# Counting two token tiles in one matmul inside a greedy expert search, on one Trainium2 core

## The chip, the cores and the metric

The kernel runs on one core of one Trainium2 chip. The metric is the device time of one launch in microseconds (us). TensorE (PE) runs matmuls, VectorE (DVE) and ScalarE (ACT) move and combine data, GpSimd (POOL) issues the gathers and scatters, SyncE (SP) the weight loads.

## The reference

```
def _attn_ref(q, k, v):            # B, H, S, D = 4, 8, 768, 64
    ...                            # window of 16 around each token, and 24 block summaries
    return np.matmul(a, v_all)

def _moe_ref(x, w_gate, w1, w2):   # N, D, E, F = 3072, 512, 8, 1024
    cap = N // E
    logits = x @ w_gate
    flat = logits.flatten()
    order = np.argsort(-flat)
    for idx in order:
        tok, e = (int(idx) // E, int(idx) % E)
        if assigned[tok] >= 0 or counts[e] >= cap:
            continue
        assigned[tok] = e
        counts[e] += 1
        ...
    for e in range(E):
        mask = assigned == e
        h = np.maximum(x[mask] @ w1[e], 0.0)
        out[mask] = h @ w2[e]
```

Attention feeds a gate. The gate hands all token and expert pairs out in the order of their logits until each of the 8 experts has its 384 tokens. Then each expert runs its two layers over its tokens.

## The kernel before

**Stages.** Attention with the logits takes the first 133 us. Then the greedy assignment is done in eight rounds (`route`, rounds 0 to 7): each round finds the next expert that fills up, and which tokens it gets. Round 0 runs alone, ahead of the first expert. Rounds 1 to 7 are interleaved with the matmuls of experts 0 to 5.

**A search.** A round (but for the last) finds the key at which the first expert is full, digit by digit: `search` runs twice, three digits each, so six digits a round and 42 in all. For one digit, VectorE compares the keys of the 24 tiles of 128 tokens with `n` (32 or 64) pivots into `g` (line 106). TensorE counts: for each tile one matmul with 128 columns of `g` as weights and the tile's one-hot experts `oh` (8 columns) as the moving operand, all 24 added up in PSUM `pc` (line 467), pivots on partitions, experts on columns. VectorE marks what has reached the capacity, with the row's maximum beside it, in `full` (line 469), a product with `steps` (line 472) turns this into the next digit, and VectorE makes the next pivots `piv` (line 476) and `g`. After the six digits come `inc`, a prefix product (lines 540 and 541), `span`, a product that lists the tokens (line 572), and `idx`, the list from which GpSimd gathers the tokens' rows (line 623, tile `xg`).

**An expert.** First 96 matmuls `h` of 128x384 (line 778): eight slices `f`, each of three groups of four, the first group with `xh` and `ah`, the second with `xh` and `al`, the third with `xl` and `ah`. Then 72 matmuls `y` of 128x512 (line 795). An operand is split in two halves so that two fast products carry its precision: `ah` and `bh` by ScalarE from the weights `raw` (line 609), `al` and `bl` by VectorE (line 612), likewise `xh` (ScalarE, line 643) and `xl` (VectorE, line 646) from the gathered rows, which TensorE transposes first (line 134, three matmuls of one of four parts `d`; below "a flip"). `hh` and `hl` (lines 782 and 785) are the halves of `h`. The flips and `h` share a pool of four PSUM buffers, so slice 0 of an expert takes the buffer of flip 0 and waits until `xh` and `xl` of part 0 have been read from it. The first `h` group of slice 0 needs `xh` of all four parts, the third group `xl` of all four.

**Order.** The program is written out by one loop over the matmuls, which keeps an estimated time `now` and an estimate of when VectorE will be free. A search step `yield`s two numbers, its cost to `now` and the time VectorE needs before the next step may be written; `vector` adds the latter to VectorE's estimate, to which the splits add theirs, and `service` writes the next step after the first matmul at which the estimate has passed. `prepare` writes the next expert's splits and flips between the `y` matmuls (`q` counts them in threes, 1 to 24): a flip once a set time has gone by since the gather, or from `q` = 22, and at `q` = 24 all that is left. All engines run their own instructions in the written order.

```
    def vector(cost):
        state["dve"] = max(state["dve"], state["now"] + TUNE["hop"]) + TUNE["dv"] * cost
        return state["dve"]
...
        if q and p["a"] < 4 and p["w"] is not None and now >= p["last"] and (q > TUNE["ql"] or now >= p["w"] + TUNE["aw"] + TUNE["as_"] * p["a"]):
            split_w(r, "a", p["a"])
...
        elif q > TUNE["qf"] and p["d"] < 4 and p["x"] is not None and (q > TUNE["ql"] or now >= max(p["x"] + TUNE["xw"], p["flip"])):
            flip_x(r, p["d"])
```

Of the kernel before, what the change touches and what calls it, by code (L numbers as in the profile page):

```python
# [8 lines left out]
F32 = mybir.dt.float32  # L9
F32R = mybir.dt.float32r  # L10
BF = mybir.dt.bfloat16
# [4 lines left out]
OP = mybir.AluOpType  # L16
AX = mybir.AxisListType
# [3 lines left out]
BLK, WIN, E, F, DM = 32, 16, 8, 1024, 512  # L21
N = B * S
CAP = N // E
# [9 lines left out]
NT = N // 128  # L33
VD = D + 1
TUNE = dict(
    hop=0.22, dv=1.0, e5=2, e50=0, warm2=3.6192, adv=14, y0=2.6, y1=0.3, y2=0.45,
    y2m=0.021, y3=1.7, y4=1.5, y5=1.6, y7=1.1, lo=1.1, sp=1.6, qx=23.421, aw=9.0, as_=2.6,
    ap=1.6, qf=8.3981, xw=5.4012, fp=2.4, ql=21.2102, mm=0.174, my=0.228, wlo=1.6, xlo=1.1, LA=6.154, PT=7, 
    sm=4, spe=0.015, sdve=0.316, sact=0.358, spool=0, m=0.569, e=2.793, t=2.307, c=0.793,
    n=0.518, xt=3.377, xf=3.104, l=5.806, k=18.109, q=16.26, vm=5, mx=12.906, back=6.52, w=5.302, qa=-11.877, qb=1.082, cut=22,  # L40
# [15 lines left out]
def attention_moe(ctx, tc, qT, kT, v65, wg, w1r, w2r, cst, out, dbg=None, dbi=None):  # L56
    nc = tc.nc
# [18 lines left out]
    rt = ctx.enter_context(tc.tile_pool(name="rt", bufs=1))  # L76
# [15 lines left out]
    HT = NT // 2  # L92
# [5 lines left out]
    def steps_tile():  # L98
        G.append(G.pop(0))
        return G[-1]  # L100

    def compare(g, dup, piv, n, t0=0, t1=NT):
        for k in range(2):
            a, b = max(t0, k * HT), min(t1, (k + 1) * HT)
            if a < b:
                nc.vector.tensor_tensor(g[k][:, (a - k * HT) * n:(b - k * HT) * n].rearrange("p (t j k) -> p t j k", k=2, j=n // 2),  # L106
                                        dup[:, a:b, None].to_broadcast([128, b - a, n // 2, 2]),
                                        piv[:, None, :n].to_broadcast([128, b - a, n]).rearrange("p t (j k) -> p t j k", k=2), op=OP.is_ge)
# [71 lines left out]
    with ExitStack() as att:  # L180
# [134 lines left out]
        for u in range(U):  # L315
            b, i = divmod(u, NQ)
            t, s = divmod(u, 2)
# [56 lines left out]
        for t in range(NT):  # L374
# [63 lines left out]
            if t + 1 in cuts:  # L438
                k = cuts.index(t + 1)
# [19 lines left out]
    nc.gpsimd.tensor_tensor(slot, ids_b[:, :3, 0], ids_b[:, :3, 1], op=OP.add)  # L459
    nc.gpsimd.tensor_scalar(slot, slot, 1.0, None, op0=OP.add)  # L460

    def search(R, oh, dup, g, digits):
        below = -32768.0 - 65536.0 / digits[0]
        for i, n in enumerate(digits):
            pc = R[:, :E]
            for t in range(NT):
                nc.tensor.matmul(pc, g[t // HT][:, t % HT * n:t % HT * n + 128], oh[:, t], start=t == 0, stop=t == NT - 1)  # L467
            full = rt.tile([128, E + 1], BF, name="full", bufs=2)
            nc.vector.tensor_scalar(full[:, :E], pc, CAP - 0.5, 0.0, op0=OP.is_ge, op1=OP.max, accum_out=full[:, E:])
            yield 0.027 * NT, TUNE["y1"]  # L470
            ps = R[:, 16:17 + E]
            nc.tensor.matmul(ps, steps[:, STEP[digits][i]], full, start=True, stop=True)
            if i < 2:
                m = digits[i + 1]
                piv = rt.tile([128, 64], I16, name="piv", bufs=2)
                nc.vector.tensor_scalar(piv[:, :m], offs[:, FROM[digits][i]:FROM[digits][i] + m], ps[:, E:], below, op0=OP.add, op1=OP.add)
                g = steps_tile()
                compare(g, dup, piv, m)
                below = rt.tile([128, 1], F32, name="below", bufs=2)
                nc.vector.tensor_scalar(below, piv[:, :1], -STEPS[STEP[digits][i + 1]][0], None, op0=OP.add)  # L480
                yield 0.03, TUNE["y2"] + m * TUNE["y2m"]
        return (below, ps[:, E:]), ps[:, :E], ps[:, E:]
# [3 lines left out]
    def route(r):  # L486
# [11 lines left out]
        if r < E - 1:  # L498
            at, won, top = yield from search(R, oh, T["dup"], T["g"], T["digits"])
            d = rt.tile([128, NT], F32, name="d", bufs=2)  # L500
            nc.vector.tensor_scalar(d, halves[:, :, 1], *at, op0=OP.subtract, op1=OP.subtract)
            nc.vector.scalar_tensor_tensor(d, d, 65536.0, halves[:, :, 0], op0=OP.mult, op1=OP.add)
            dup2 = rt.tile([128, NT, 2], I16, name="dup", bufs=2)
            nc.vector.tensor_scalar(dup2, d[:, :, None].to_broadcast([128, NT, 2]), 32767.0, -32768.0, op0=OP.min, op1=OP.max)
            g = steps_tile()
            compare(g, dup2, piv0, 32)
            wh = rt.tile([128, E], F32, name="wh", bufs=2)
            nc.vector.scalar_tensor_tensor(wh, won, top, w8f, op0=OP.is_equal, op1=OP.mult)
            yield 0.03, TUNE["y3"]
            at, won, top = yield from search(R, oh, dup2, g, EVEN)  # L510
            wl = rt.tile([128, E], F32, name="wl", bufs=2)
            nc.vector.scalar_tensor_tensor(wl, won, top, wh, op0=OP.is_equal, op1=OP.mult)
            nc.vector.tensor_scalar(d, d, *at, op0=OP.subtract, op1=OP.subtract)
            nc.vector.tensor_reduce(w, wl, axis=AX.X, op=OP.max)
            sel = rt.tile([128, NT], F32, name="sel", bufs=2)
            nc.vector.tensor_scalar(sel, tgt, w, None, op0=OP.is_equal)
            nc.vector.tensor_scalar(widx, w[:1], -512.0, 512.0 * E, op0=OP.mult, op1=OP.add)
            nc.vector.scalar_tensor_tensor(ge[:, 0], d, 0.0, sel, op0=OP.is_gt, op1=OP.mult)
            nc.vector.scalar_tensor_tensor(ge[:, 1], d, 0.0, sel, op0=OP.is_equal, op1=OP.mult)
        else:  # L520
            nc.vector.tensor_scalar(w, wsum, -1.0, float(E * (E + 1) // 2), op0=OP.mult, op1=OP.add)
            nc.vector.tensor_scalar(ge[:, 0], tgt, w, None, op0=OP.is_equal)
            nc.vector.tensor_scalar(widx, w[:1], -512.0, 512.0 * E, op0=OP.mult, op1=OP.add)
            nc.vector.memset(ge[:, 1], 0.0)
# [350 lines left out]
```

## Time and profile before

| | us |
|---|---|
| median of 3 runs | 487.07 (486.86 to 488.96) |
| the profiled execution | 486.22 |
| span of its instructions | 484.5 |
| TensorE busy | 451.9 |
| VectorE busy | 335.0 |

The span runs from the first instruction to the last; 1.7 us of the execution lie around it. Busy time of TensorE is from modelled ends, so a matmul that waits inside a stream can still be counted as busy. A row of the timeline gives the start, the duration, the engine and line, and in brackets the idle time of the engine before it and what ended it; rows of one kind that follow each other are merged with their count, and then the duration runs from the first start to the last end.

### The profile page before, as it was taken

To read this page: it belongs to the slowest core of one execution; us is meant where nothing else is said; L and a number is where in the kernel's file an instruction comes from. 1 tells how busy PE (TensorE), PEld (TensorE's weight loads), DVE (VectorE), ACT (ScalarE), POOL (GpSimd) and SP (SyncE) were. 2 spreads that over 40 slices of the span, in tenths; PEclk is the share of its full clock that TensorE was granted. 3 is DMA by queue.
4 is the path that set the end of the run, shared out by engine and by line. 5 is a ranking of instruction groups with operands and counts; after the bars stand their busy time and mean duration, and the time that the engine had idled before them with its cause. 6 is when DMAs were issued, how large, how long until landed. Compare 5 with 4: busy or idle time off the path is not lost.

```text
span 484.5 us, 13157 instructions
## 1 busy us (share of the span) xinstructions
PE 451.9 (93%) x5159; PEld 382.8 (79%) x5159; DVE 335.0 (69%) x1307; ACT 215.1 (44%) x449; POOL 126.6 (26%) x209
## 2 busy tenths in 40 slices
PE   6999999999946899999989999999999999999992
PEld 5686877878835797798779779878878988989981
DVE  5989889869768877768858947876877661562500
ACT  3886877858401432433234324514342453443400
POOL 2597839224113001300221112104101302202010
PEclk9999999999955999999999999999999999999998
DMA  8998392211204704703715606605525662621001
GB/s 303 410 330 312 118 375 84 78 46 67 90 3 141 272 2 167 277 37 141 271 68 179 236 23 227 229 2 200 195 86 197 179 225 99 174 85 66 0 23 43
DMA packets 22429, 73.38 MB, mean 151 GB/s; under 512 B 3168, under 2 KB 3424, under 8 KB 21984
## 3 DMA queue, kind: packets, MB, share of 16 engines
q1 hardware_dynamic: 16608, 53.67, 31.6%
q0 software_dynamic: 5760, 18.88, 11.1%
q8 instruction: 41, 0.67, 0.6%
q14 instruction: 20, 0.16, 0.1%
HBM read 59.95 MB, written 12.58 MB: 150 GB/s over the span
## 4 chain that ended last, share of the span: by engine, by line
PE 75%; DVE 11%; issue 7%; DMA 2%; POOL 2%; SPq 1%; ACT 1%; POOLq 0%; DVEq 0%; ACTq 0%
PE y L795 23%; PE h L778 22%; PE o L366 5%; PE r L467 5%; PE t L134 5%; PE s L330 4%; PE x L134 3%; PE l L372 3%; PE h L134 2%; DMA vw<-v 1%; DVE g L106 1%; POOL out L761 1%; DVE bl L612 1%; DMA xg<-xd,idx 1%; PE x L272 1%
## 5 line engine op out<-in xcount | busy, mean ns | idle before, releaser
L795 PE MATMUL y<-bl,hh 128*128 128x512 f32 x192 | 77.9, 406 | 0.0
L795 PE MATMUL y<-bh,hh 128*128 128x512 f32 x192 | 77.0, 401 | 0.0
L795 PE MATMUL y<-bh,hl 128*128 128x512 f32 x192 | 76.4, 398 | 0.0
L761 POOL DMA_INDIRECT out<-y,idx x24 | 24.1, 1006 | 181.5 <-ACT y L759 175.1
L782 ACT ACTIVATE hh<-h 128x384 fp32r<-128x384 f32 x64 | 31.5, 492 | 88.3 <-PE h L778 86.8
L778 PE MATMUL h<-xh,ah 128*128 128x384 f32 x256 | 57.2, 341 | 0.9 <-DVE xl L749 0.9
L345 ACT ACTIVATE pe<-sm,mx 128x120 f32<-128x120 f32 x192 | 57.9, 386 | 0.3 <-DVE mx L338 0.2
L778 PE MATMUL h<-xl,ah 128*128 128x384 f32 x256 | 57.8, 341 | 0.0
L778 PE MATMUL h<-xh,al 128*128 128x384 f32 x256 | 57.1, 340 | 0.0
L785 DVE SCALAR_TENSOR_TENSOR hl<-h,hh 128x384 fp32r<-128x384 f32 x64 | 35.1, 551 | 29.2 <-ACT hh L782 28.4
L623 POOL DMA_INDIRECT xg<-xd,idx x24 | 23.7, 987 | 106.8 <-issue 79.6
L609 ACT ACTIVATE ah<-raw 128x1024 fp32r<-128x1024 f32 (+1 forms) x36 | 32.7, 958 | 34.6 <-DMA raw<-w1r 33.9
L778 PEld LDWEIGHTS h<-xh,ah 128*128 128x128 f32 x256 | 45.0, 188 | 2.2 <-DVE xl L749 1.1
L778 PEld LDWEIGHTS h<-xl,ah 128*128 128x128 f32 x256 | 45.0, 188 | 2.1 <-issue 1.6
L643 ACT ACTIVATE xh<-h 128x384 fp32r<-128x384 f32 x28 | 13.7, 492 | 72.1 <-PE h L134 72.0
L778 PEld LDWEIGHTS h<-xh,al 128*128 128x128 f32 x256 | 45.1, 188 | 0.0
L338 DVE CUSTOM_DVE_ANT_0 sm<-s,cs 128x120 f32<-128x120 f32 x192 | 41.2, 278 | 4.8 <-PE s L330 4.3
L467 PEld LDWEIGHTS <-g 128*128 128x128 bf16 x1008 | 28.7, 97 | 18.4 <-DVE g L106 7.7
L795 PEld LDWEIGHTS y<-bh,hh 128*128 128x128 f32 x192 | 36.2, 188 | 6.5
L795 PEld LDWEIGHTS y<-bl,hh 128*128 128x128 f32 x192 | 36.2, 188 | 6.0 <-issue 0.5
L795 PEld LDWEIGHTS y<-bh,hl 128*128 128x128 f32 x192 | 36.2, 189 | 5.8
L467 PE MATMUL r<-oh,g 128*128 128x8 bf16 x1008 | 32.5, 167 | 7.3 <-DVE g L106 3.8
(137 smaller groups left out, 790.9 us busy)
## 6 DMA issues: line engine op xcount, KB each, us to landing
raw<-w1r SPq DMA_DIRECT2D x32, 512.0 KB
raw<-w2r SPq DMA_DIRECT2D x32, 512.0 KB, 4.3
kd<-kT SPq DMA_DIRECT2D x16, 400.0 KB, 5.4
vw<-v SPq DMA_DIRECT2D x24, 260.0 KB, 7.5
xd<-x POOLq DMA_DIRECT2D x24, 256.0 KB
qt<-qT SPq DMA_DIRECT2D x3, 1536.0 KB
qt<-qT SPq DMA_DIRECT2D x3, 512.0 KB
xg<-xd,idx POOLq DMA_INDIRECT x24
```

What stands on the lines that cost most here:

```text
L134: nc.tensor.transpose(o, i, idn)
L338: nc.vector.tensor_tensor_reduce(sm[:, p], PS[u][:, p], m, -0.125, 3e38, op0=OP.add, op1=OP.min, accum_out=mx[:, p:p + 1])
L345: nc.scalar.activation(PE_[u][:, p], SM[u][0][:, p], AF.Exp, bias=SM[u][1][:, p:p + 1], scale=-1.0)
L366: nc.tensor.matmul(po(t, s)[x * 64:x * 64 + 64, p], PT[u][:, p, x * 64:x * 64 + 64], VW[b % 2][:C, i - s + x, 2 * p + s], start=True, stop ...
L467: nc.tensor.matmul(pc, g[t // HT][:, t % HT * n:t % HT * n + 128], oh[:, t], start=t == 0, stop=t == NT - 1)
L609: nc.scalar.activation(hi[:, c], raw[:, c], AF.Copy)
L623: nc.gpsimd.indirect_dma_start(out=x, out_offset=None, in_=xd, in_offset=bass.IndirectOffsetOnAxis(ap=idx[:, c:c + 1], axis=0))
L761: st = nc.gpsimd.indirect_dma_start(out=out, out_offset=bass.IndirectOffsetOnAxis(ap=ROUND[r][1][:, c:c + 1], axis=0), in_=y, in_offset=None)
L778: nc.tensor.matmul(ph, a[:, d], b[:, d], start=n == 0, stop=n == 11)
L782: nc.scalar.activation(hh[:, f], ph, AF.Relu)
L785: nc.vector.scalar_tensor_tensor(hl[:, f], ph, 0.0, hh[:, f].bitcast(F32), op0=OP.max, op1=OP.subtract)
L795: nc.tensor.matmul(py[c], a[:, f, s], b, start=f == 0 and i == 0, stop=f == 7 and i == 2)
```

## The change

One count matmul now takes two tiles: the weights are, as before, 128 columns of `g`, which hold the pivots of two tiles (with 32 pivots, of four, of which two count), and the moving operand is `oh` of both tiles, 16 columns. The sum of 12 matmuls has the wanted counts in two diagonal blocks: partitions 0 to n and columns 0 to 8 for the even tiles, partitions n to 2n and columns 8 to 16 for the odd ones. VectorE adds them in the comparison: it reads the second block at partition n and writes `short` (capacity less that count) at partition 0, compares the first block with it, and reduces to the row's maximum. `pc` moves to other columns of the same PSUM tile, and `full` becomes two fixed tiles that GpSimd clears once. The planner's numbers of the step change too: its cost from 0.027 to 0.017 a tile (0.648 to 0.408 us in all), VectorE's time `y1` from 0.3 to 0.5 us.

```diff
-    hop=0.22, dv=1.0, e5=2, e50=0, warm2=3.6192, adv=14, y0=2.6, y1=0.3, y2=0.45,
+    hop=0.22, dv=1.0, e5=2, e50=0, warm2=3.6192, adv=14, y0=2.6, y1=0.5, y2=0.45,
...
+    fulls = [rt.tile([128, E + 1], BF, name=f"full{k}") for k in range(2)]
+    for full in fulls:
+        nc.gpsimd.memset(full, 0.0)
+
     def search(R, oh, dup, g, digits):
         below = -32768.0 - 65536.0 / digits[0]
         for i, n in enumerate(digits):
-            pc = R[:, :E]
-            for t in range(NT):
-                nc.tensor.matmul(pc, g[t // HT][:, t % HT * n:t % HT * n + 128], oh[:, t], start=t == 0, stop=t == NT - 1)
-            full = rt.tile([128, E + 1], BF, name="full", bufs=2)
-            nc.vector.tensor_scalar(full[:, :E], pc, CAP - 0.5, 0.0, op0=OP.is_ge, op1=OP.max, accum_out=full[:, E:])
-            yield 0.027 * NT, TUNE["y1"]
+            pc = R[:, 384:384 + 2 * E]
+            for t in range(0, NT, 2):
+                nc.tensor.matmul(pc, g[t // HT][:, t % HT * n:t % HT * n + 128], oh[:, t:t + 2].rearrange("p t e -> p (t e)"), start=t == 0, stop=t == NT - 2)
+            fulls.append(fulls.pop(0))
+            full = fulls[-1]
+            short = rt.tile([64, E], F32, name="short", bufs=2)
+            nc.vector.tensor_scalar(short[:n], pc[n:2 * n, E:], -1.0, CAP - 0.5, op0=OP.mult, op1=OP.add)
+            nc.vector.tensor_tensor(full[:n, :E], pc[:n, :E], short[:n], op=OP.is_ge)
+            nc.vector.tensor_reduce(full[:n, E:], full[:n, :E], axis=AX.X, op=OP.max)
+            yield 0.017 * NT, TUNE["y1"]
```

Lines after the change lie 4 to 8 lower (471 counts, 475 to 477 are `short`, the comparison and the maximum, 480 the product, 484 `piv`, 786 `h`, 803 `y`).

**VectorE at the first digit of round 0**, a part of the difference between the two programs:

```order
-L469 TENSOR_SCALAR full<-r 128x8
-L476 TENSOR_SCALAR piv<-cs,r 128x32
+L475 TENSOR_SCALAR short<-r 64x8
+L476 TENSOR_TENSOR full_2940<-r,short 64x8
+L477 TENSOR_REDUCE full_2940<-full_2940 64x1
+L484 TENSOR_SCALAR piv<-cs,r 128x32
 L106 TENSOR_TENSOR g_79<-dup,piv 128x384
 L106 TENSOR_TENSOR g_80<-dup,piv 128x384
```

One instruction (which the chip runs as two, with the read of the accumulator) becomes three, each of which reads what the one before wrote.

**TensorE at the change from expert 2 to expert 3**, where the last `y` of expert 2 meets the first `h` of expert 3. Before:

```order
L795 MATMUL y<-bh,hl 128x512
L472 LDWEIGHTS steps
L472 MATMUL r<-full,steps 128x9
L795 MATMUL y<-bh,hh 128x512
L778 MATMUL h<-xh,ah 128x384 x4
L778 MATMUL h<-xh,al 128x384 x4
```

And of the change:

```order
L134 MATMUL h<-cs,xg 128x128 x3
L803 MATMUL y<-bl,hh 128x512
L480 LDWEIGHTS steps
L480 MATMUL r<-full_2941,steps 128x9
L803 MATMUL y<-bh,hl 128x512
L803 MATMUL y<-bh,hh 128x512
L803 MATMUL y<-bl,hh 128x512
L803 MATMUL y<-bh,hl 128x512
L803 MATMUL y<-bh,hh 128x512
L134 MATMUL h<-cs,xg 128x128 x9
L786 MATMUL h<-xh,ah 128x384 x4
```

Before, the four flips of expert 3 stand after 30, 39, 48 and 57 of the 72 `y` matmuls of expert 2. Now one stands after 66 and three after all 72. At the other changes it is so: 0 to 1 had them after 60, 66 and twice 72, 1 to 2 after 48, 57, 66 and 69, 3 to 4 and 4 to 5 after 30, 39, 48, 57, 5 to 6 after 27, 39, 51, 63. Now all of 0 to 1, 1 to 2, 2 to 3, 3 to 4, 4 to 5 have them after 66 and three times 72, 5 to 6 after 63, 69 and twice 72; 6 to 7 is as it was. The last product of a digit (line 480) ahead of each of the first five changes stands after 67 of the 72, the listing product (line 580) in each of experts 0 to 5 after 32 or 33, in experts 0 to 4 the two counts behind it after 51 or 52 and 61 or 62, their products after 55 or 56 and 67.

**VectorE at the same place.** Before:

```order
L612 TENSOR_TENSOR al<-raw,ah 128x1024 x2
L469 TENSOR_SCALAR full<-r 128x8
L612 TENSOR_TENSOR al<-raw,ah 128x1024
L476 TENSOR_SCALAR piv<-cs,r,below 128x64
L106 TENSOR_TENSOR g_77<-dup,piv 128x768
L106 TENSOR_TENSOR g_78<-dup,piv 128x768
L480 TENSOR_SCALAR below<-piv 128x1
L646 TENSOR_TENSOR xl<-h,xh 128x384 x2
```

And of the change:

```order
L484 TENSOR_SCALAR piv<-cs,r,below 128x64
L106 TENSOR_TENSOR g_77<-dup,piv 128x768
L106 TENSOR_TENSOR g_78<-dup,piv 128x768
L488 TENSOR_SCALAR below<-piv 128x1
L620 TENSOR_TENSOR al<-raw,ah 128x1024
L654 TENSOR_TENSOR xl<-h,xh 128x384
L620 TENSOR_TENSOR al<-raw,ah 128x1024
L654 TENSOR_TENSOR xl<-h,xh 128x384
L620 TENSOR_TENSOR al<-raw,ah 128x1024
L654 TENSOR_TENSOR xl<-h,xh 128x384 x2
```

Before, all four `al` stand ahead of the pivots or nearly so, and `xl` of the first two parts follow. Now three `al` and all four `xl` stand behind the pivots, which wait for the product after `y` 67. ScalarE's order there is now `ah` twice, `xh`, `y`, `ah`, `y`, `xh`, `ah`, `xh` twice, `y` (before: `ah` four times, `xh` four times, `y` three times), where `y` is the copy of an output tile out of PSUM (line 759).

## Rows read from the trace of the kernel before

**Rows 1.** The page's head and its first section: busy time of each engine, share of the span, instructions.

```profile
span 484.5 us, 13157 instructions
...
PE 451.9 (93%) x5159; PEld 382.8 (79%) x5159; DVE 335.0 (69%) x1307; ACT 215.1 (44%) x449; POOL 126.6 (26%) x209
```

**Rows 2.** Windows: start and end, length, then busy time of each engine with its instructions, the granted clock (PEclk, 1.00 is 2.4 GHz, 0.50 is 1.2 GHz), DMA share and GB/s. The first row is round 0 with the start of expert 0, the others run from the first `h` matmul of an expert to that of the next, experts 0 to 6.

```profile
133.00:158.00 25.00, 13.71 (x256) 11.73 (x253) 17.96 (x89) 2.25 (x4) 5.77 (x10) 0.59 0.24 75
161.62:203.92 42.30, 41.88 (x393) 35.80 (x394) 31.66 (x101) 15.98 (x25) 4.20 (x7) 1.00 0.46 169
203.92:245.30 41.38, 41.27 (x348) 34.61 (x347) 31.70 (x101) 15.65 (x25) 5.72 (x9) 1.00 0.40 142
245.30:289.20 43.90, 42.23 (x395) 35.80 (x394) 31.87 (x106) 15.61 (x24) 7.02 (x12) 1.00 0.37 133
289.20:331.08 41.88, 41.46 (x372) 35.02 (x371) 31.51 (x107) 15.24 (x24) 6.53 (x10) 1.00 0.40 139
331.08:372.93 41.85, 40.81 (x360) 34.92 (x359) 33.81 (x117) 15.10 (x24) 7.16 (x11) 1.00 0.56 189
372.93:407.86 34.93, 34.93 (x190) 31.47 (x189) 17.69 (x33) 15.18 (x24) 6.52 (x11) 1.00 0.52 166
407.86:442.33 34.47, 34.47 (x181) 31.32 (x180) 15.86 (x20) 15.28 (x24) 6.53 (x11) 1.00 0.35 107
```

**Rows 3.** Timeline of TensorE in expert 1: a count of 24 matmuls, the `h` matmuls behind it.

```profile
215.15 0.76 PE L467 MATMUL r<-oh,g 128*128 128x8 bf16 x24
215.77 0.60 PE L778 MATMUL h<-xh,al 128*128 128x384 f32 x2
216.21 0.34 PE L778 MATMUL h<-xl,ah 128*128 128x384 f32 x1
```

**Rows 4.** Timeline of TensorE later in expert 1: the listing product, 12 matmuls of 128x128 weights with 25 moving columns.

```profile
226.81 0.46 PE L572 MATMUL r<-place,span 128*128 128x25 f16 x12
```

**Rows 5.** Timeline of TensorE and VectorE in round 0: a digit with 32 pivots, from the count to the product.

```profile
138.72 0.81 PE L467 MATMUL r<-oh,g 128*128 128x8 bf16 x24 [0.79 <-DVE g L106]
...
139.57 0.17 DVE L469 TENSOR_SCALAR_CACHE_REDUCE full<-r 128x8 bf16<-128x8 f32 x1 [0.57 <-PE r L467]
...
139.80 0.17 PE L472 MATMUL r<-full,steps 128*128 128x9 bf16 x1 [0.27 <-DVE full L469]
```

**Rows 6.** Groups by line and shape: busy us and mean ns of one, then the idle time before them.

```profile
L392 DVE TENSOR_SCALAR dn<-o 128x4 f32<-128x4 f32 x48 | 6.8, 156 | 4.9 <-PE o L366 4.9
...
L512 DVE SCALAR_TENSOR_TENSOR wl<-r,wh 128x8 f32<-128x8 f32 x7 | 1.6, 226 | 2.4 <-PE r L472 2.4
...
L548 DVE TENSOR_TENSOR to<-r,inc 128x2 f32<-128x2 f32 x8 | 1.2, 152 | 0.0
...
L514 DVE TENSOR_REDUCE w<-wl 128x1 f32<-128x8 f32 x7 | 1.1, 153 | 0.0
```

**Rows 7.** Waits of TensorE between 155 and 372 us: what waited for what, us in total, times, the longest.

```profile
PE r L472 <- DVE full L469: 2.8, 4, 1.6
PE r L467 <- DVE oh L127: 1.0, 1, 1.0
```

**Rows 8.** Timeline of VectorE at the change from expert 0 to expert 1.

```profile
199.87 0.32 DVE L476 TENSOR_SCALAR piv<-cs,r,below 128x64 int16<-128x64 f32 x1 [1.22 <-PE r L472]
...
201.23 1.22 DVE L612 TENSOR_TENSOR al<-raw,ah 128x1024 fp32r<-128x1024 f32 x1
202.36 0.55 DVE L646 TENSOR_TENSOR xl<-h,xh 128x384 fp32r<-128x384 f32 x1
202.83 1.22 DVE L612 TENSOR_TENSOR al<-raw,ah 128x1024 fp32r<-128x1024 f32 x1
...
204.51 1.22 DVE L612 TENSOR_TENSOR al<-raw,ah 128x1024 fp32r<-128x1024 f32 x1
205.65 1.01 DVE L646 TENSOR_TENSOR xl<-h,xh 128x384 fp32r<-128x384 f32 x2
```

**Rows 9.** Timeline of ScalarE at the same change.

```profile
201.45 0.49 ACT L643 ACTIVATE xh<-h 128x384 fp32r<-128x384 f32 x1 [0.37 <-PE h L134]
201.84 0.59 ACT L759 ACTIVATE y<-y 128x512 f32<-128x512 f32 x1
202.32 1.06 ACT L609 ACTIVATE ah<-raw 128x1024 fp32r<-128x1024 f32 x1
203.26 0.60 ACT L759 ACTIVATE y<-y 128x512 f32<-128x512 f32 x1
203.88 0.87 ACT L643 ACTIVATE xh<-h 128x384 fp32r<-128x384 f32 x2
```

**Rows 10.** Timeline of TensorE at the same change: the digit's product, two flips, the first `h` group, and the first matmul of slice 1.

```profile
199.63 0.18 PE L472 MATMUL r<-full,steps 128*128 128x9 bf16 x1
...
203.35 0.82 PE L134 MATMUL h<-cs,xg 128*128 128x128 f32 x6
203.92 1.32 PE L778 MATMUL h<-xh,ah 128*128 128x384 f32 x4
...
206.99 0.34 PE L778 MATMUL h<-xh,ah 128*128 128x384 f32 x1
```

**Rows 11.** Timeline of TensorE at the change from expert 5 to expert 6: the first `h` group of slice 0 and the first matmul of slice 1.

```profile
407.86 0.87 PE L778 MATMUL h<-xh,ah 128*128 128x384 f32 x4
...
409.96 0.33 PE L778 MATMUL h<-xh,ah 128*128 128x384 f32 x1
```

## Prediction

> **What bounds the kernel now.** The totals come first: TensorE is busy 451.9 of 484.5 us [rows 1], so it is the engine to follow, but a share of the whole span says nothing of one stage. The windows by stage tell two stages of interest apart [rows 2]. In round 0 TensorE has 13.7 busy us of 25 and the clock is down to 0.59 on average; there the chain between TensorE and VectorE sets the time. From expert 0 on TensorE is full. Expert 6, which hosts no search, takes 34.47 us from its first matmul to that of expert 7; experts 0 to 4, which host searches, take 42.30, 41.38, 43.90, 41.88 and 41.85. Between 161.62 and 442.33 us a matmul that leaves TensorE's stream is time saved, and a wait of TensorE is time lost. The list of waits [rows 7] says how little it waits there now: 2.8 us for `full` and 1.0 us for `oh`. The change of expert 0 to 1 [rows 8 to 10] is the one place where more than that shows, and the change 5 to 6 [rows 11] is how it looks without it.
>
> **The count.** 24 matmuls keep the next `h` back by 215.77 - 215.15 = 0.62 us [rows 3], 25.8 ns each. What is a matmul of 16 moving columns worth? The count has 8, and the listing product has 25 with weights of the same 128 columns: 12 in 0.46 us, less some 0.17 us for the end of the last, is 0.29 / 11 = 26 ns [rows 4]. 16 lies between 8 and 25, so I take 25.8 ns; both bounds are the same. The `h` behind a count comes 0.44 us later for two where 0.35 is normal [rows 3, 11], a loss of 0.09 us at each break, which stays. Rounds 1 to 6 have 36 digits, one of them ahead of expert 0. 35 digits x 12 matmuls x 25.8 ns = **10.8 us saved**.
>
> **The three VectorE instructions, and round 0.** Now the result of the count reaches the product 0.23 us after VectorE starts on it, 0.06 of it the way from VectorE's end to TensorE [rows 5]. The forms of `short` and of the comparison do not stand in this trace with a read at another partition. The nearest rows are 0.156 us for a scalar operation on 4 columns of PSUM and 0.152 for a tensor operation on 2, the maximum over 8 columns takes 0.153, and the dearest of this size is 0.226 [rows 6]. With 0.16, 0.15 and 0.15, each of the three reading what the one before wrote, and three ways of 0.06, it is 0.64 us: 0.41 more a digit (0.37 with three times 0.15 and ways of 0.05, 0.63 with three times 0.226). In round 0 this is on the path, six times: +2.5. Against it the count there, 24 in 0.81 us [rows 5], or 27.8 ns each, could give 0.33 us a digit, but it starts on the first half of `g` while VectorE still makes the second, so I take 0.2 on average: -1.2. Net **+1.3 us** (0.9 to 2.9).
>
> A page gives these instructions another price. The Trainium skill (VectorE: DVE Perf Modes, section on the TRN2 errata) puts a VectorE instruction at 120 cycles of 0.96 GHz plus its elements from PSUM, and 58 plus elements from SBUF. For 8 elements that makes 0.133, 0.133 and 0.069 us, and round 0 would cost about +0.5 us, an estimate by that page. The rows nearest to them are longer (0.152 to 0.156), so the sum goes by the rows.
>
> Within the experts the same 0.41 us a digit is cover: the product stands behind at least four `y` matmuls or eight `h`. An `h` takes 2.10 / 12 = 0.175 us [rows 11]. Of expert 6's 34.47, 72 `y` have what 96 x 0.175 leaves, 17.7, less four flips (six thirds and six thirds: 203.92 - 203.35 = 0.57 us for two flips [rows 10], so 0.29 each): 0.229 each. Four of them and a break are 1.0 us. The chain needs 0.17 for the last count and 0.64. It fits by 0.2 us where VectorE is free when the count ends.
>
> **What moves: the expert changes.** This is where the gain goes, by my sum. The planner's new numbers bring each round to its list 40 matmuls ahead of the expert that needs it, in every expert alike, so that the flips are written last: one after `y` 66, three after `y` 72. Let T be the end of `y` 72. VectorE's new pivots wait for the product after `y` 67, that is until about T - 5 x 0.229 - 0.1 + 0.24 = T - 1.0 (0.24 from 199.63 to 199.87 [rows 8, 10]). Behind them in VectorE's order stand `al`, `xl`, `al`, `xl`, `al`, `xl`, `xl`. The very same sequence runs at the change 0 to 1 now: from 199.87 until 205.65 + 1.01 = 206.66, 6.8 us [rows 8], of which I leave out 0.1 for a `full` that stands among them: 6.7. So the last `xl` ends at T + 5.7, and slice 0, whose last matmul reads it, at T + 5.9. ScalarE alone would end it little earlier: from start to start `xh` takes 0.39, an output copy 0.48 and `ah` 0.94 [rows 9]; flip 0 begins behind `y` 66 at T - 1.8 and hands over 0.53 later (203.35 to 203.88 [rows 9, 10]), at T - 1.3, and `xh`, `y`, `ah`, `y`, `xh`, `ah`, `xh`, `xh` end at T + 3.2, so that slice 0 could end at T + 5.2. Unhindered it would be three flips 0.86, 2.10, and a count of 12 with its break 0.4: T + 3.4. The wait is 2.5 us by VectorE, at least 1.8 by ScalarE.
>
> That it works so shows at the change 0 to 1 now: the pivots come 3.5 us ahead of the last flips, the last `xl` 3.3 us behind 203.35, and slice 0 takes 206.99 - 203.92 = 3.07 us, where 2.10 and a product of 0.13 would do: 0.84 us lost [rows 8, 10, 11]. In the change the pivots stand 2.5 us later against T, and so does the end.
>
> Five changes (0 to 1 up to 4 to 5) x 2.5 = 12.5. At 5 to 6 no pivots are in the way, but two flips stand at the end and two `ah` ahead of the last two `xh`: the same rows give the last `xl` at about T + 4.9 against T + 2.7 unhindered, 2.3 us. Sum 14.8, less what is lost at these places now (0.84, and about 0.1 at 1 to 2): **+13.9 us** (9.0 by a wait of 1.8 at five changes and 0.9 at the sixth, 16 with half a microsecond more at four).
>
> **What goes away.** The waits of 2.8 and 1.0 us [rows 7] come from products written three `h` or `y` behind their count, and from counts written before `oh` was ready. Now a product has four `y` or eight `h` ahead of it. I leave 0.5 of the 3.8: **-3.3 us** (0 to -3.8).
>
> **Sum.** -10.8 + 1.3 + 13.9 - 3.3 = +1.1 us on the profiled execution's 486.22: 487.3. The median of the runs lies 0.85 us above that execution, so 488.0 by the median, no difference that can be told: I count 0.5%, 2.4 us, as what a measurement of this kernel can tell from no change.
>
> **The rivals.**
> - **The changes of expert cost half as much** (chance 0.28). If ScalarE and VectorE clear their queues ahead of T more than I see, and the wait is some 1.2 us a change, 7 us come off: 481.0, faster. For it speaks that VectorE is busy only some 32 us of 42 in these experts [rows 2], so that it has time to catch up before T. Against it: what stands behind the pivots cannot start before them, whatever time was free earlier. With no wait at all it would be 474.
> - **VectorE's chain no longer fits ahead of the product** (0.22). If a read at another partition than the write makes the three instructions 0.32 us each, as long as the pivots' [rows 8], the chain is 0.96 + 0.18 + 0.17 = 1.3 us against 1.0 us at the two products of a round that stand four to six `y` behind their count, in five experts: +3; round 0 takes 6 x 0.5 = +3 more. 494, slower. It decides from the point where three instructions and their ways exceed 0.8 us. Against it: nothing in the rows of this size is over 0.23 but operations with two operands of a value a partition.
> - **The change does not save TensorE time** (0.04): if 16 columns take twice what 8 do, the 10.8 us are not there: 499. Rows 4 speak against it.
>
> My sum has 0.46: what is won in the stream is lost at the changes. Of it 0.02 reach past +0.5%. So faster by over 0.5% has 0.28, within 0.5% 0.44, slower 0.28. The range: the first rival spreads from 474 to 484, and a third of it (0.09) lies under 479.5; above 495.5 lie a third of the second (0.07) and the third rival (0.04). That leaves 0.2 outside 479.5 to 495.5.
>
> **What would show it.** Right: the count rows have 12 matmuls and keep the next `h` back by 0.31 us; in experts 1 to 4 slice 0 ends 5 to 6 us after `y` 72, with the three flips and a count in it; TensorE's waits name `xl` and `xh`, 14 us in all in place of 3.8; experts 1 to 4 take about 41 us each; round 0 is about 1 us longer. Wrong: experts 1 to 4 at 38 to 39 us, with no such waits, would mean that the first rival holds; waits for `full` in every round, the second; a count of 12 in 0.6 us, the third.

## The result, and the profile after

The changed kernel takes 490.79 us (median of 7 runs, 488.66 to 491.94), the kernel before 487.07: a ratio of 1.006 (1.0031 to 1.0088), 3.7 us slower. The forecast was 488.0, in a range of 479.5 to 495.5. The profiled execution has a span of 488.7 us against 484.5. The page's head and busy times, which answer to [rows 1]:

```profile
span 488.7 us, 12165 instructions
...
PE 449.5 (92%) x4655; PEld 374.2 (77%) x4655; DVE 348.8 (71%) x1349; ACT 212.7 (44%) x449; POOL 129.8 (27%) x211
```

TensorE has 504 matmuls less and is busy only 2.4 us less; VectorE has 13.8 us more. The windows by stage, which answer to [rows 2] (round 0, then experts 0 to 6 from first `h` to first `h`; PEclk stands third from the end):

```profile
133.00:158.00 25.00, 9.35 (x141) 7.96 (x142) 16.27 (x86) 1.08 (x2) 4.00 (x10) 0.55 0.15 48
164.29:204.54 40.25, 39.36 (x286) 33.29 (x286) 33.00 (x108) 15.36 (x24) 4.94 (x8) 1.00 0.47 171
204.54:245.48 40.94, 39.71 (x272) 32.91 (x272) 31.41 (x99) 14.89 (x24) 7.09 (x11) 1.00 0.41 149
...
368.36:408.27 39.91, 39.06 (x254) 32.41 (x255) 28.81 (x92) 13.40 (x23) 6.13 (x9) 1.00 0.39 141
408.27:446.53 38.26, 36.63 (x184) 32.75 (x182) 19.84 (x26) 17.61 (x27) 7.19 (x11) 0.96 0.46 169
```

Experts 0 to 4 became shorter (40.25 and four times 40.95). Expert 5 is longer (39.91 for 34.93), since the last four digits now fall into it, and so is expert 6 (38.26 for 34.47), which hosts none: it begins with a wait. From the first `h` of expert 0 to that of expert 7 it is 282.24 us against 280.71: +1.5. Expert 0 itself starts 2.7 us later (164.29 against 161.62); 0.4 of that lies ahead of the first count of round 0 (134.00 against 133.56).

TensorE's waits between 155 and 420 us, which answer to [rows 7]:

```profile
PE h L786 <- DVE xl L654: 3.6, 4, 0.9
PE h L786 <- ACT xh L651: 2.6, 6, 1.6
...
PE h L786 <- DVE al L620: 0.9, 1, 0.9
```

No wait for `full` is left; `h` waits for `xl` and `xh` instead. The change 2 to 3 on TensorE, then on VectorE, which answer to [rows 10] and [rows 8]; T, where the flips behind the last `y` start, is 284.41:

```profile
284.41 1.15 PE L134 MATMUL h<-cs,xg 128*128 128x128 f32 x9
286.45 0.62 PE L786 MATMUL h<-xh,ah 128*128 128x384 f32 x2 [0.89 <-DVE xl L654]
287.25 0.82 PE L786 MATMUL h<-xh,ah 128*128 128x384 f32 x2 [0.18 <-ACT xh L651]
287.91 0.46 PE L471 MATMUL r<-oh,g 128*128 128x16 bf16 x12
288.23 0.94 PE L786 MATMUL h<-xh,al 128*128 128x384 f32 x4
289.01 1.55 PE L786 MATMUL h<-xl,ah 128*128 128x384 f32 x4
290.39 0.68 PE L786 MATMUL h<-xh,ah 128*128 128x384 f32 x3
```

```profile
283.35 0.32 DVE L484 TENSOR_SCALAR piv<-cs,r,below 128x64 int16<-128x64 f32 x1 [0.92 <-PE r L480]
...
284.71 1.21 DVE L620 TENSOR_TENSOR al<-raw,ah 128x1024 fp32r<-128x1024 f32 x1
285.84 0.55 DVE L654 TENSOR_TENSOR xl<-h,xh 128x384 fp32r<-128x384 f32 x1
286.31 1.21 DVE L620 TENSOR_TENSOR al<-raw,ah 128x1024 fp32r<-128x1024 f32 x1
287.44 0.55 DVE L654 TENSOR_TENSOR xl<-h,xh 128x384 fp32r<-128x384 f32 x1
287.91 1.21 DVE L620 TENSOR_TENSOR al<-raw,ah 128x1024 fp32r<-128x1024 f32 x1
289.04 1.01 DVE L654 TENSOR_TENSOR xl<-h,xh 128x384 fp32r<-128x384 f32 x2
```

The count of 12 keeps the next `h` back by 288.23 - 287.91 = 0.32 us (0.62 in [rows 3]). The last `xl` ends at 290.05, T + 5.64, and slice 1 starts at 290.39, T + 5.98.

Round 0 on VectorE and GpSimd, which answers to [rows 5]: the first digit, a later one, and what GpSimd does ahead of `full`:

```profile
135.64 0.17 DVE L475 TENSOR_SCALAR short<-r 64x8 f32<-64x8 f32 x1 [0.33 <-PE r L471]
138.10 0.16 DVE L476 TENSOR_TENSOR full<-r,short 64x8 bf16<-64x8 f32 x1 [2.30 <-POOL full L464]
...
142.34 0.16 DVE L475 TENSOR_SCALAR short<-r 32x8 f32<-32x8 f32 x1 [0.36 <-PE r L471]
142.54 0.15 DVE L476 TENSOR_TENSOR full<-r,short 32x8 bf16<-32x8 f32 x1
142.72 0.15 DVE L477 TENSOR_REDUCE full<-full 32x1 bf16<-32x8 bf16 x1
```

```profile
135.88 1.54 POOL L455 TENSOR_SCALAR count<-colsi 128x128 f16<-128x128 int16 x3 [3.98 <-DMA xd<-x]
...
137.96 0.15 POOL L464 MEMSET full<- 128x9 bf16 x2
```

The product of the later digit starts at 142.93, so the chain takes 0.59 us where it took 0.23 in [rows 5]. At the first digit there is a wait of 2.30 us that the prediction does not have: the clearing of `full` stands in GpSimd's queue behind `count`, which waits for a transfer. From the first count to the first product it is 4.51 us (134.00 to 138.51), against 2.24 before (133.56 to 135.80). The wait is not the same in every execution: where `count` starts at 134.80 or 136.28 in place of 135.88 (the work alone, the second run with added matmuls), the first product starts at 137.47 or 138.91, 2.6 to 2.7 us behind it each time.

### The profile page after: what moved, and what is told of

It reads as the page before. It is cut to its first block, busy times and chain, and to the rows that moved or that the text cites. A ratio compares the mean times of both kernels' runs of the same rounds, so it can differ in the third digit from the quotient of the medians.

```text
span 488.7 us, 12165 instructions
## 1 busy us (share of the span) xinstructions
PE 449.5 (92%) x4655; PEld 374.2 (77%) x4655; DVE 348.8 (71%) x1349; ACT 212.7 (44%) x449; POOL 129.8 (27%) x211
## 4 chain that ended last, share of the span: by engine, by line
PE 70%; issue 13%; DVE 10%; DMA 3%; POOL 2%; ACT 1%; POOLq 0%; SPq 0%; DVEq 0%
PE h L786 21%; PE y L803 20%; PE o L366 6%; PE s L330 5%; PE t L134 5%; DVE al L620 4%; PE x L134 3%; PE l L372 3%; PE r L471 3%; DVE g L106 1%; POOL out L769 1%; DVE xl L654 1%; PE x L272 1%; PE y L739 1%; DMA xd<-x 1%
## 5 line engine op out<-in xcount | busy, mean ns | idle before, releaser
L803 PE MATMUL y<-bl,hh 128*128 128x512 f32 x192 | 76.9, 401 | 0.0
L617 ACT ACTIVATE ah<-raw 128x1024 fp32r<-128x1024 f32 (+1 forms) x36 | 34.0, 965 | 83.6 <-DMA raw<-w1r 65.6
L786 PE MATMUL h<-xh,ah 128*128 128x384 f32 x256 | 60.4, 350 | 8.1 <-DVE xl L654 3.6
L786 PE MATMUL h<-xl,ah 128*128 128x384 f32 x256 | 61.1, 347 | 0.7
L769 POOL DMA_INDIRECT out<-y,idx x24 | 29.6, 1233 | 98.8 <-ACT y L767 92.4
L620 DVE TENSOR_TENSOR al<-raw,ah 128x1024 fp32r<-128x1024 f32 (+1 forms) x36 | 38.9, 1097 | 0.6 <-ACT ah L617 0.6
L620 DVE TENSOR_TENSOR bl<-raw,bh 128x1024 fp32r<-128x1024 f32 x32 | 38.9, 1215 | 0.0
L617 ACT ACTIVATE bh<-raw 128x1024 fp32r<-128x1024 f32 x32 | 33.7, 1053 | 1.0 <-DMA raw<-w2r 1.0
```

The lines of the kernel that those rows point to most:

```text
L617: nc.scalar.activation(hi[:, c], raw[:, c], AF.Copy)
L620: nc.vector.tensor_tensor(lo[:, c], raw[:, c], hi[:, c].bitcast(F32), op=OP.subtract)
L769: st = nc.gpsimd.indirect_dma_start(out=out, out_offset=bass.IndirectOffsetOnAxis(ap=ROUND[r][1][:, c:c + 1], axis=0), in_=y, in_offset=None)
L786: nc.tensor.matmul(ph, a[:, d], b[:, d], start=n == 0, stop=n == 11)
L803: nc.tensor.matmul(py[c], a[:, f, s], b, start=f == 0 and i == 0, stop=f == 7 and i == 2)
```

## The experiments

Times are medians; a ratio is to the kernel before on the same chip, with its interval. Two groups of runs were on chips where the kernel before takes 487.6 and 488.0 us, the other two groups on chips where it takes 483.9 and 483.2.

**1. The two halves of the change, each alone.** First only the planner's numbers, in the kernel before:

```diff
-    hop=0.22, dv=1.0, e5=2, e50=0, warm2=3.6192, adv=14, y0=2.6, y1=0.3, y2=0.45,
+    hop=0.22, dv=1.0, e5=2, e50=0, warm2=3.6192, adv=14, y0=2.6, y1=0.5, y2=0.45,
...
-            yield 0.027 * NT, TUNE["y1"]
+            yield 0.017 * NT, TUNE["y1"]
```

> The kernel before with only the planner's two numbers of the change (cost 0.017 a tile, y1 0.5): 24 count matmuls a digit and one comparison as before, but flips, counts and products in the order of the changed kernel. My theory (the order costs what the work wins): +13.9 - 3.3 = +10.6 us by the sum of the prediction, to +12 by the experts of the changed kernel; round 0 stays as before: 497.5 to 499 us, with a wait of 2 to 2.5 us at each of the changes 0 to 1 up to 4 to 5 and 3 to 4 us at 5 to 6. Rival 1: the changes cost half as much, 493. Rival 2: the order costs nothing and the work won nothing, 487.

Measured: 500.91 us, ratio 1.0277 (1.0222 to 1.0332), 13.3 us slower. Its experts 1 and 4, by windows:

```profile
204.56:248.45 43.89, 42.58 (x345) 36.27 (x345) 29.49 (x93) 14.90 (x24) 7.09 (x11) 0.96 0.37 132
...
336.26:379.01 42.75, 41.48 (x344) 34.78 (x344) 29.50 (x93) 14.85 (x24) 7.15 (x11) 1.00 0.37 136
```

Experts 1 to 3 (43.89, 43.89 and 43.92) do the same work in the same order as expert 4 and take 1.15 us longer; in them PEclk is 0.96, not 1.00: behind the wait at their start the granted clock is at 0.50 for a stretch. From expert 0 to expert 7 this kernel takes 294.89 us, 14.2 more than before; without the three falls, 3.5 us, it is 10.7, and my sum for the order was 10.6.

Then the work alone, in the order of the kernel before:

```diff
-    hop=0.22, dv=1.0, e5=2, e50=0, warm2=3.6192, adv=14, y0=2.6, y1=0.5, y2=0.45,
+    hop=0.22, dv=1.0, e5=2, e50=0, warm2=3.6192, adv=14, y0=2.6, y1=0.3, y2=0.45,
...
-            yield 0.017 * NT, TUNE["y1"]
+            yield 0.027 * NT, TUNE["y1"]
```

> The changed kernel with the planner's two numbers of before (cost 0.027 a tile, y1 0.3): 12 count matmuls and three VectorE instructions, but flips, counts and products in the order of the kernel before. My theory: -10.8 us by the count, +1.3 and +2.3 in round 0 (the chain, the clearing of `full`), and some +3 at products that stand three matmuls behind their count and now wait 0.4 longer: 487.1 - 4.2 = 483 us (481 to 485). Rival 1: the matmul saving is not there, 492 or more. Rival 2: all products are covered, 480.

Measured: 480.33 us, ratio 0.9855 (0.9829 to 0.988): 7.1 us less by the ratio, the second rival's figure, though not its reason, since waits for `full` of 2.3 us are left. Experts 0 to 5 take 238.35 us against 246.24, 7.9 less where the count alone gives 10.8. So the work alone pays, and the planner's numbers cost more than it pays. The two halves add up to +6.2 us, the whole change is +3.7: the order alone has three falls of the clock in its profile, the whole change one, which is 2 us of the difference. One place where the longer chain takes something back is the change 0 to 1, where it stands among the splits (VectorE, then TensorE):

```profile
204.43 0.17 DVE L475 TENSOR_SCALAR short<-r 64x8 f32<-64x8 f32 x1
...
206.50 1.01 DVE L654 TENSOR_TENSOR xl<-h,xh 128x384 fp32r<-128x384 f32 x2
```

```profile
207.10 0.91 PE L786 MATMUL h<-xl,ah 128*128 128x384 f32 x2 [0.42 <-DVE xl L654]
```

**2. The clearing of `full`.** Moved to GpSimd's start, all else as in the changed kernel:

```diff
     for pair in G:
         for g in pair:
             nc.gpsimd.memset(g, 0.0)
+    fulls = [rt.tile([128, E + 1], BF, name=f"full{k}") for k in range(2)]
+    for full in fulls:
+        nc.gpsimd.memset(full, 0.0)
```

> The changed kernel with one edit: the two `full` tiles are cleared at the start of GpSimd's work, behind the tiles `g`, and no longer behind `count`, which waits for the rows of `x`. Order of all else as in the changed kernel. My theory: the first comparison of round 0 no longer waits 2.3 us for the clearing, round 0 is shorter by 2.3 us, the experts stay as they are: 490.8 - 2.3 = 488.5 us. Rival: the 2.3 us lie beside another wait of round 0 (GpSimd's or a DMA's), and the time stays at 490.8.

Measured: 491.1 us, ratio 1.0073 (1.0049 to 1.0097): nothing won, and not by the rival's reason. The 2.3 us of the expectation are those of one execution: from the first count to the first product it is 2.67 to 4.51 us in the eight profiles with the clearing behind `count`, 2.24 to 2.37 in the four with `full` cleared early, so 0.4 to 2.2 us are to be had. Round 0 did get shorter: the wait of 2.30 is gone and expert 0 starts at 162.49, 1.8 earlier. But experts 0, 1, 3 and 4 are 0.8 longer each, with a wait that the changed kernel's list does not have (first row); the other rows are VectorE, TensorE and GpSimd at expert 1:

```profile
PE r L479 <- DVE full L476: 2.9, 4, 0.7
```

```profile
237.74 0.16 DVE L474 TENSOR_SCALAR short<-r 32x8 f32<-32x8 f32 x1 [1.69 <-PE y L802]
```

```profile
236.11 0.46 PE L470 MATMUL r<-oh,g 128*128 128x16 bf16 x12
```

```profile
235.96 0.95 POOL L630 DMA_INDIRECT xg<-xd,idx  x1 [0.30 <-issue]
```

The count ends at 236.57, and `short`, which needs nothing else (the row names a later `y`), starts at 237.74. In the profiled execution of the changed kernel the same instruction, at the same place in the same order, started 0.37 behind its count. The last section comes back to this. The clock also fell at the change 4 to 5 here and not at 5 to 6.

**3. One number of the planner.**

```diff
-    hop=0.22, dv=1.0, e5=2, e50=0, warm2=3.6192, adv=14, y0=2.6, y1=0.5, y2=0.45,
+    hop=0.22, dv=1.0, e5=2, e50=0, warm2=3.6192, adv=14, y0=2.6, y1=0.45, y2=0.45,
```

> The changed kernel with one number changed, the planner's VectorE time of a count step y1, from 0.5 to 0.45. The rounds now get ahead of the experts: flips after 60, 66, 72, 72 of the 72 `y` at 0 to 1, 57, 66, 72, 72 at 1 to 2, 51, 60, 66, 69 at 2 to 3, and 27 to 57 from there on (in the changed kernel 66, 72, 72, 72 at all of them). My theory: the waits at the changes go from 2.5 us each to 0.9, 1.5, 0.1, 0, 0 and from 3.8 to 0, -14 us, and waits for `full` come back with about 3 us: 480 us (478 to 483). Experts 2 to 4 take about 39 us in place of 41. Rival (the products' waits eat what the changes give): 488 or more.

Measured: 478.59 us, ratio 0.9803 (0.9776 to 0.9831), as expected. Experts 3 and 4, by windows:

```profile
286.75:326.18 39.43, 39.07 (x287) 33.13 (x285) 33.02 (x108) 15.62 (x24) 7.42 (x11) 1.00 0.42 147
326.18:365.59 39.41, 39.15 (x287) 33.08 (x285) 33.04 (x108) 15.12 (x24) 7.53 (x11) 1.00 0.43 148
```

The same 12 matmuls and three VectorE instructions a digit, flips of these experts after 27 to 57 of the `y` in place of 66 and 72: 1.5 us less an expert, with seven digits in each of them where the changed kernel has six. With y1 0.5 every round comes to its list at the same matmul of each expert; with 0.45 each comes some matmuls earlier than the last, and the flips leave the end.

**4. What holds the change of expert.** VectorE's `xl` ahead of `al`:

```diff
-                later.append((state["now"] + wait, low))
+                later.append((state["now"] + wait, low, nm == "a"))
...
-        for it in later[:]:
+        for it in sorted(later, key=lambda it: len(it) > 2 and it[2]):
```

> The changed kernel; where the splits that are left are written out at the start of an expert, VectorE's `xl` now stand ahead of `al` (behind the pivots: `al`, four `xl`, two `al`, in place of `al`, `xl`, `al`, `xl`, `al`, `xl`, `xl`). TensorE's and ScalarE's order and the planner's numbers stay. My theory (the last `xl` is late because of the pivots and the `al` ahead of it): the last `xl` goes from T + 5.6 to T + 3.7, where ScalarE's last `xh` (T + 3.15) bounds it, slice 0 ends at T + 4.1 in place of T + 6.0; 1.9 us at five changes, nothing at 5 to 6, where ScalarE is late: 490.8 - 9.4 = 481.4 (480 to 484). Rival: ScalarE's queue or another wait takes the place of `xl`, under 3 us are won: 488 or more.

Measured: 490.58 us, ratio 1.004 (1.0015 to 1.0065): my figure missed. TensorE at the change 1 to 2, T = 244.37, and the windows of experts 1 and 2:

```profile
246.42 0.62 PE L786 MATMUL h<-xh,ah 128*128 128x384 f32 x2 [0.91 <-DVE xl L654]
247.22 0.82 PE L786 MATMUL h<-xh,ah 128*128 128x384 f32 x2 [0.18 <-ACT xh L651]
...
249.69 0.85 PE L786 MATMUL h<-xh,ah 128*128 128x384 f32 x4
```

```profile
204.58:246.42 41.84, 40.69 (x272) 34.51 (x273) 31.51 (x99) 14.90 (x24) 7.40 (x11) 0.96 0.39 142
246.42:286.71 40.29, 39.20 (x273) 32.96 (x273) 31.42 (x99) 14.85 (x24) 7.43 (x11) 1.00 0.39 141
```

Slice 1 starts at T + 5.3: behind the last `xh` TensorE still has the end of the first group, a count and two groups to do. That is the T + 5.2 which the prediction gives for ScalarE alone; in this expectation I had left those groups out. VectorE's share of the wait is thus 0.65 us (40.29 for 40.95). And at 0 to 1, 2 to 3 and 4 to 5 the clock fell (PEclk 0.96), which took back 1.5 us each.

With the flips also written ahead of the `ah` that are left:

```diff
         if q == 24:
-            while p["a"] < 4:
-                split_w(r, "a", p["a"])
-                p["a"] += 1
             while p["d"] < 4:
                 flip_x(r, p["d"])
                 p["d"] += 1
+            while p["a"] < 4:
+                split_w(r, "a", p["a"])
+                p["a"] += 1
```

> As the run before, and the flips that are left when the expert ends are written ahead of the `ah` that are left, so that ScalarE's last `xh` stand ahead of the last `ah`. My theory: the last `xh` ends at T + 2.2, the last `xl` at T + 3.5 by VectorE (pivots to T + 0.5, `al` to T + 1.65, four `xl`), slice 0 ends at T + 3.8, where T + 3.4 is unhindered; at 5 to 6 two `ah` leave the way, 1.9 us, and the fall of the clock behind them, 1.5: 490.8 - 11 - 3.4 = 476.4 (475 to 479). Rival: the `al` that are now last hold slice 2 or 4 back, 482.

Measured: 482.92 us, ratio 0.9906 (0.9879 to 0.9933), 7.7 us less than the run before; the clock never fell, and experts 1 to 3 take 39.6. At the change 1 to 2, T = 243.49:

```profile
245.54 0.98 PE L786 MATMUL h<-xh,ah 128*128 128x384 f32 x4 [0.90 <-DVE xl L654]
...
248.18 0.85 PE L786 MATMUL h<-xh,ah 128*128 128x384 f32 x4
```

Slice 1 starts at T + 4.7; what is left is slice 0's wait of 0.9 for the first `xl`, which pivots and one `al` hold back. I had 476.4, counted from the end of the last `xl`: the sum left out that slice 0 starts behind the first `xl` and then has a count and three groups to do.

**5. Is it the wait that lowers the clock?** The run with `xl` first, with matmuls that compute nothing needed in its wait:

```diff
     def expert(r):
         flush()
+        if 0 < r < E - 1:
+            fill = psum.tile([128, DM], F32, name="y", bufs=3)
+            for _ in range(14):
+                nc.tensor.matmul(fill[:, :128], upper_b, upper_b, start=True, stop=True)
```

> The kernel with `xl` ahead of `al`, and 14 added matmuls of 128x128 bf16 (of a constant, into a PSUM buffer that nobody reads) at the start of experts 1 to 6, behind the flips, where TensorE waits 0.9 us for the first `xl`. They are no part of the computation. In that kernel the granted clock fell to 0.50 for 3.4 us behind the changes 0 to 1, 2 to 3 and 4 to 5, whose experts took 41.8, 41.8 and 40.9 us, and not behind 1 to 2 and 3 to 4, with 40.3. My theory (the clock falls because TensorE stands idle at the change): the falls go, experts 1, 3 and 5 are 1.4 to 1.5 us shorter, 490.6 - 4.4 = 486.2. Rival: the clock falls for another reason, or the added matmuls take as much as they give: 490.6 or more.

> The kernel with the 14 added matmuls once more, on a chip as it comes. In its first run the falls of the clock were gone and the experts 4.9 us shorter together, as my theory had it, but the kernel before was itself 4 us faster on that chip, so that the ratio stayed at 1.004. My theory: beside a kernel before of 487 to 488 it takes 486 to 487, a ratio of 0.996 to 0.999. Rival: the ratio is 1.004 again, and what the fall of the clock costs in the trace is given back somewhere else.

Measured: 486.67 and 485.73 us, ratios 1.004 (1.0017 to 1.0063) and 1.0041 (1.0022 to 1.006). In both profiles PEclk is 1.00 in every expert from 1 to 6; the first one's experts 1 and 3:

```profile
205.48:245.70 40.22, 39.83 (x286) 33.70 (x287) 31.41 (x99) 14.89 (x24) 7.39 (x11) 1.00 0.41 141
...
286.16:326.50 40.34, 40.01 (x286) 33.68 (x287) 31.40 (x99) 14.83 (x24) 7.40 (x11) 1.00 0.40 148
```

1.6 and 1.4 us less than without the added matmuls, and no more in the experts in which the clock had not fallen (40.46 and 40.26 for 40.29 and 40.34). The four profiles with these waits and without the added matmuls (the changed kernel, `full` cleared early, the order alone, `xl` first) have one, one, three and three falls at their six changes, the two with them none: that TensorE's idle time brings the falls is likely by this, though two profiles are few for something that comes and goes. The Trainium skill (TensorE: Matmul & The Clock Gate, section on HAM oscillation) tells the same of kernels whose TensorE waits between bursts. The time does not show the gain: the kernel takes 3.9 and 4.9 us less than with `xl` first, but on these two chips the kernel before takes 4.1 and 4.8 us less as well, so that the ratio is 1.004 in all three runs, as the rival of the second run had it. What the added matmuls give in time on one chip is open: the two kernels were not run on the same one.

**6. Together.** The two edits of order with y1 0.45, and then with `full` cleared early:

> The two edits of order together with y1 0.45. With y1 0.45 alone it was 478.6 us, with waits of some 1.8 us left at 0 to 1 and 1.1 at 1 to 2, where flips still stand behind the last `y`. My theory: these go, 478.6 - 2 = 476.6. Rival: they come from something else than `al` and `ah`, 478.6.

> As the run before, and `full` cleared at the start of GpSimd's work. My theory: round 0 is shorter by the 1.8 us that expert 0 started earlier when this was done to the changed kernel: 474.8. Rival, as that run showed: VectorE's first comparison of a round starts 0.8 us later at some experts and takes it back, 476.6.

Measured: 476.66 us, ratio 0.9777 (0.9741 to 0.9813), and 476.18, ratio 0.9775 (0.9748 to 0.9803), the lowest ratio of all. Clearing early gives nothing that can be told; expert 0 starts 1.6 earlier in that profile and expert 4's search waits 0.9 for `full`. Smaller y1 on top of it:

> The fastest kernel so far (y1 0.45, `xl` and `xh` first, `full` cleared early: 476.2 us) with y1 0.3. Flips after 60, 69, 72, 72 at 0 to 1, 51, 60, 66, 69 at 1 to 2, and 27 to 57 from 2 to 3 on; products stand nearer to their counts. My theory: the waits at the changes are gone already and the products' waits for `full` grow by some 1 to 2 us: 477.5. Rival: the earlier flips of 2 to 3 give 0.5 us a change more, 475.5.

> The same with y1 0.2: flips after 57, 66, 72, 72 at 0 to 1, 36 to 63 at 1 to 2, and 27 to 60 from then on, products nearer still. My theory: waits for `full` grow by 2 to 3 us, 478.5. Rival: 475.5.

Measured, on a chip where the kernel before takes 483.91: 475.23, ratio 0.9821 (0.9796 to 0.9846), and 477.41, ratio 0.9861 (0.9836 to 0.9887). Whether 0.3 is better or worse than 0.45 can't be told: 475.23 us is the lower time, 0.9775 the lower ratio, and y1 0.45 was not run on a chip where the kernel before takes 484. That 0.2 is worse than 0.3 is shown on one chip, by 2.2 us. The reason I gave is not what their profiles show: no wait for `full` is listed in either, and with y1 0.2 it is expert 1 that is long again, 41.5 us, with TensorE waiting 0.3 us for `xl` at its start and 1.0 us for `xg` at a flip.

## Why the prediction was right or wrong

- **The count: right.** 0.32 us in place of 0.62, at 16 columns as at 8, and in the experiments the matmuls saved are worth what the sum has: the changed kernel is 12.65 us shorter in the experts than the kernel with its order and 24 matmuls (282.24 against 294.89): about the 10.8 of the count and the 2 us by which one fall of the clock costs less than three.
- **The three instructions: right.** 0.16, 0.15 and 0.15 us, 0.59 for the chain where I had 0.64. A read at another partition costs nothing that shows (0.157 us for `short` on 32 rows, 0.156 in [rows 6] without the shift), and the rival that rests on it falls.
- **Round 0: the step failed.** It priced the chain and left out where the new tiles are cleared. The change adds two instructions to GpSimd's queue behind `count`, and the first comparison waits 2.30 us for them. From the first count of round 0 to the first `h` of expert 0 it is 30.28 us in place of 28.06, +2.2 where the forecast was +1.3; with `full` cleared early it is 28.09, as before. The chain itself costs about what it was priced at: from the first product to the sixth it is 12.05 us in place of 11.22, 0.17 a digit net of the count, for 0.21. But from the sixth product to expert 0, where a digit of round 1 stands, 0.9 us come back (13.73 in place of 14.60), which the forecast did not have. Its bounds, 0.9 and 2.9, come out of its own figures as 1.0 and 2.6.
- **The changes 0 to 1 to 4 to 5: right.** T + 5.64 for the last `xl` and T + 5.98 for slice 0 (5.7 and 5.9), experts 1 to 4 at 40.95 (about 41). The rival with half the wait falls. The sign of 14 us in TensorE's list of waits did not come: the list has 7.1 us for `xl`, `xh` and `al` (3.6, 2.6 and 0.9). A part of the rest lies inside the stream: the four `h` with `xl` at 289.01 take 1.55 us, where four take 0.85 in the fourth experiment. That ScalarE alone would hold slice 0 until T + 5.2 was right as well, and it was the part that I forgot when I put numbers to the fourth experiment.
- **The change 5 to 6: too small.** 2.3 us was the forecast, and expert 6 takes 38.26 in place of 34.47. The wait for `xh` behind two `ah` is as long as thought, but the clock fell behind it:

```profile
408.06 2.01 ACT L617 ACTIVATE ah<-raw 128x1024 fp32r<-128x1024 f32 x2
```

```profile
410.50 0.82 PE L786 MATMUL h<-xh,ah 128*128 128x384 f32 x2 [1.63 <-ACT xh L651]
...
412.99 1.48 PE L786 MATMUL h<-xh,ah 128*128 128x384 f32 x4
414.26 1.42 PE L786 MATMUL h<-xh,al 128*128 128x384 f32 x4
```

  That expert 6 in the run with 24 matmuls in the same order takes 36.90 without a fall puts it at 1.4 us.
- **The waits that go: right in this profile.** No wait for `full` is left. But the fit is as narrow as forecast, 0.2 us: at expert 1 `short` starts 0.37 us behind its count and the product does not wait, and with `full` cleared early, where it starts 1.17 behind, the waits are back with 2.9 us in four experts. That VectorE's start could be held up so was no term of the prediction.
- **The sum.** For the experts it was -10.8 + 13.9 - 3.3 = -0.2 and came out at +1.5, of which 1.4 is the clock; for round 0 +1.3 and came out at +2.2, with 0.4 more ahead of it. The two terms that are missing, the clearing (2.3) and the clock (1.4), are 3.7 of the 4.2 us by which the profiled span grew, and turn "no change that can be told" into 0.6% slower; in the medians the clearing does not show, since the run without it is no faster. The prediction gave its own sum a chance of 0.02 to end past 0.5% slower, so the measured 0.6% (0.3% to 0.9%) is near its figure but past what it held likely. That figure has a slip: 486.22 + 1.1 + 0.85 is 488.2, not 488.0. The large terms stood, and the conclusion drawn from them, that the order takes back what the count gives, is shown by the two halves of the change: +13.3 and -7.1 us.

## What to carry to other kernels

Cost a planner's number like an instruction: look at where each moved item lands relative to the point where its consumer starts, on every engine that feeds it, and try the neighbouring values, since 0.45 in place of 0.5 turned this change from 0.6% slower into 2% faster. Of a tile that is now filled once, ask which queue fills it and what stands ahead of it there. A wait of two microseconds on TensorE may cost half as much again by the clock behind it.

## What the hardware showed that was not expected

**VectorE's late start.** On two of the four chips of the experiments the first comparison of a round, released while GpSimd issues the third gather of `xg`, starts no earlier than the end of that issue, and in some executions 0.8 to 0.9 us later still (the rows of the second experiment). The trace of the kernel before has such a start, 0.98 us behind its count:

```profile
194.05 0.95 POOL L623 DMA_INDIRECT xg<-xd,idx  x1 [0.30 <-issue]
...
195.94 0.17 DVE L469 TENSOR_SCALAR_CACHE_REDUCE full<-r 128x8 bf16<-128x8 f32 x1 [1.81 <-PE y L795]
```

On the other two chips it starts at once. GpSimd and VectorE there, in the second run with added matmuls:

```profile
236.62 0.94 POOL L631 DMA_INDIRECT xg<-xd,idx  x1 [0.30 <-issue]
```

```profile
237.27 0.16 DVE L475 TENSOR_SCALAR short<-r 32x8 f32<-32x8 f32 x1 [0.56 <-PE r L471]
```

The count ended at 237.24, in the middle of the issue, and `short` started 0.03 us behind it. These are the two chips on which the kernel before is 4 us faster. Its products stand as little as three matmuls behind their counts, so it would feel such starts; that they are the whole of the 4 us is not shown. The Trainium skill (Trainium Architecture — The Big Picture, section on what this means for kernel authors) says that VectorE and GpSimd contend for a shared pair of ports, by an exclusive lock. A start held to the end of GpSimd's issue would fit that, but the instruction that is held reads PSUM, and no run here shows which ports it needs; the further 0.8 us, and that only some chips do it, no run here explains either. Whether the changed kernel stands worse against the kernel before on the faster two was not tried.

**The clock's fall is not certain.** With the same program and nearly the same wait, the granted clock fell at three changes of expert and not at the others, and where it falls differs between kernels that wait alike: at 0 to 1, 2 to 3 and 4 to 5 with `xl` first, at 0 to 1, 1 to 2 and 2 to 3 with 24 matmuls, at none of these five in the changed kernel. It falls to 0.50, 1.2 GHz, and `h` takes 0.32 us in place of 0.175 (four of them from 412.99 to 414.26). Ahead of expert 0 it is alike: in five of the profiles with 12 matmuls the granted clock falls once more at 159 to 161 us, and from the sixth product of round 0 to expert 0 it is 14.9 to 15.3 us there, 13.7 to 13.8 in the other seven.
